# The second matrix product of a fused mLSTM cell and gated layer: seven half-width products in place of eight

## The chip, the cores and the metric

One core of a Trainium2 chip runs the whole program. The metric is device microseconds of one execution; the time of before is the median of three runs. Engines are named as in the profile: PE (matrix engine, with PEld for its weight loads), DVE (VectorE), ACT (ScalarE), POOL (GpSimd) and SP (the queue that issues most DMAs).

## The reference, cut to what matters

Two stages in float32. An mLSTM cell (4 batches, 8 heads, 768 steps, head size 40) gives `y`, which is laid out as `x` with 3072 rows and 320 columns. Then

```
h = x @ w_in          # (3072, 320) @ (320, 2048)
g = h * cos(h)
out = g @ w_out       # (3072, 2048) @ (2048, 320)
```

The cell is a recurrence over time; the kernel computes it in chunks of 128 steps, with a state carried from chunk to chunk. Only the last line, `g @ w_out`, is computed differently by the change. Both kernels compute it in float32.

## The kernel before

Time is cut into 6 chunks (c) of 128 steps, each for 4 batches (b). A chunk's layer has 16 blocks of 128 columns of `h` (NF = 16), two for each of 8 *slots* f2. Slot f2 = 2b + i of chunk c is one half of the body of `both_parts(c, b)`; the two slots of one b are called a pair here. In chunks 0 to 4 a pair also computes the cell of batch b for the next chunk (n = 4(c + 1) + b); chunk 5 has no cell left. In chunk 4 the cell no longer updates the state.

What PE runs in a pair, in the order in which the kernel writes it (all engines keep that order):

- first slot: `Up` (L605, L608: two tiles `pup` of 128x512 from `xT` and `w_in`), `scores` (ps, L462), `down` (po, L637), `values` (vt, L488 to L495);
- second slot: `Up`, `seam` (px, L563, which reads `yt`; and pu, L570), `down`.

`down(c, f2 - 1)` is the product with `w_out`: for two column blocks and four batches, 8 matmuls of 128x128 by 128x320, added up in four PSUM tiles `po` over the chunk. It runs one slot behind `Up`; the chunk's last one runs in the first slot of the next chunk, where ACT copies the four tiles out (L640) and SP stores them (L641).

What VectorE runs in a pair:

- first slot: L616 twice (after ACT's L613), `weigh` (L468 twice), `decay_exponents(n + 1)` (L387, followed on POOL by L388 and on ACT by the exponent L396), the gates L625 twice (they write `g` and set the `pup` tiles free), then `turn_gate` (oT, L440) and `normalize_turned` (L504 to L515), whose last instruction writes the third of `yt` that px reads;
- second slot: L616 twice, `state` (L588), the gates, then `turn_blocks` (L435 twice: `t`, which ps of the next pair reads).

POOL has besides L388: the multiplication into `xT` (L514), `fade` (L550), `weigh_k` (kw, L401) and `scale_q` (qG, L444, which values reads). ACT has L613, the sine L621, in the first pair of a chunk `sigmoid(c + 1)`, the exponents, and table loads between them.

In chunk 0 the kernel also brings in both weight matrices as 64-bit numbers and converts them to float32 on ACT, DVE and POOL (`to_float32`, L148 to L156).

```
        order = [(f, b) for f in (2 * f2, 2 * f2 + 1) for b in range(B)]
        for f, b in order:
            nc.tensor.matmul(po[c][b], gs[c, f][:, ts(b, C)], w_out_sb[:, f], start=(f == 0), stop=(f == NF - 1))
```

Of the kernel before, what the change touches and what calls it, by code (L numbers as in the profile page):

```python
# [29 lines left out]
def kernel(  # L30
# [23 lines left out]
    C = 128  # L54
# [16 lines left out]
    wp = ctx.enter_context(tc.tile_pool(name="wp", bufs=1))  # L71
    p2 = ctx.enter_context(tc.tile_pool(name="p2", bufs=2))
    p3 = ctx.enter_context(tc.tile_pool(name="p3", bufs=3))
    pe = ctx.enter_context(tc.tile_pool(name="pe", bufs=2))
    p1 = ctx.enter_context(tc.tile_pool(name="p1", bufs=1))
    pb = ctx.enter_context(tc.tile_pool(name="pb", bufs=4))
    pc = ctx.enter_context(tc.tile_pool(name="pc", bufs=3))
# [113 lines left out]
    M0 = gates.tile([BH, C], FP, name="M0")  # L191
    e0 = gates.tile([BH, C], FP, name="e0")
    nM = gates.tile([BH, 1], FP, name="nM")
    a1 = gp.tile([128, WQ], FP, name="a1", tag="g")[0:BH].rearrange("r (c s) -> r c s", c=R)
    F1 = gp.tile([128, WQ], FP, name="F1", tag="g")[0:BH].rearrange("r (c s) -> r c s", c=R)
    M1 = gp.tile([128, WQ], FP, name="M1", tag="g")[0:BH].rearrange("r (c s) -> r c s", c=R)

    keep = gp.tile([128, WQ], FP, name="keep", tag="g")[0:BH].rearrange("r (c s) -> r c s", c=R)
    shift = gp.tile([128, WQ], FP, name="shift", tag="g")[0:BH].rearrange("r (c s) -> r c s", c=R)
    m0 = gates.tile([BH, R], FP, name="m0")  # L200
    dd = gates.tile([BH, R - 1, BH], FP, name="dd")
    nc.gpsimd.memset(keep, 1.0)
# [140 lines left out]

    def load_E(n):
        c, b = divmod(n, B)
        E = pe.tile([128, 2, H, C], FP, name="E", tag="E") if n % 2 == 0 else E2[n // 2]
        if n % 2 == 0:
            E2[n // 2] = E
        if c > 0:
            src = M_d[1][b * H:(b + 2) * H, ts(c - 1, C)]  # L350
            nc.sync.dma_start(out=E.rearrange("q b h t -> q (b h) t"), in_=src.unsqueeze(0).to_broadcast([128, 2 * H, C]))
            Es[n + 1] = E[:, 1]
            G = p2.tile([128, 2 * HP, C], FP, name="G", tag="G")
            src = G_d.rearrange("(b p j) t -> j (b p) t", j=2, p=HP)
            for j in range(2):
                nc.sync.dma_start(out=G[64 * j:64 * j + 64], in_=src[j, 4 * b:4 * b + 8, ts(c - 1, C)].unsqueeze(0).to_broadcast([64, 2 * HP, C]))
            Gs[n], Gs[n + 1] = G[:, 0:HP], G[:, HP:2 * HP]
        elif n not in SPREAD:
            nc.sync.dma_start(out=E[:, n % 2], in_=M_d[0][ts(b, H)].unsqueeze(0).to_broadcast([128, H, C]))
        Es[n] = E[:, n % 2]  # L360

    E2 = {}
    pm = {}

    def wall_in(n, i, m):
# [227 lines left out]
    class Up:  # L593
# [27 lines left out]
            nc.scalar.activation(out=r, in_=r, func=AF.Sin, scale=TWO_PI_DOWN)  # L621

        def gate(self, e):
            g = gp.tile([128, WQ], FP, name="g", tag="g")[:, 0:B * C]
            nc.vector.scalar_tensor_tensor(out=g, in0=self.pu[e], scalar=TWO_PI, in1=self.n[e].bitcast(FP),  # L625
                                           op0=OP.mult, op1=OP.mult)
            gs[self.c, 2 * self.f2 + e] = g

    def down(c, f2):
        if f2 == 0:  # L630
            po[c] = [ps_o.tile([128, DM], FP, name="po", tag="o") for _ in range(B)]

        order = [(f, b) for f in (2 * f2, 2 * f2 + 1) for b in range(B)]
        if f2 == NF // 2 - 1:
            order.sort(key=lambda fb: fb[1])
        for f, b in order:
            nc.tensor.matmul(po[c][b], gs[c, f][:, ts(b, C)], w_out_sb[:, f], start=(f == 0), stop=(f == NF - 1))  # L637
            if f == NF - 1:
                o = p2.tile([128, DM], FP, name="o_sb", tag="o_sb")
                nc.scalar.copy(out=o, in_=po[c][b])  # L640
                nc.sync.dma_start(out=out[b * S + c * C:b * S + (c + 1) * C], in_=o)  # L641


    pw, pmu = (ps_u.tile([128, HP, C], FP, name=name, tag="up") for name in ("pw", "pmu"))

# [5 lines left out]
    def first_cells():  # L651
        nc.vector.memset(nil, 0.0)
        gates_in()
        nc.scalar.copy(out=ident_b, in_=ident)
        load(0, "qk")
        later_gates_in()
        load(0, "v")
        load(1, "qk")
        load_o(0, (0, 1))
        load(1, "v")  # L660
        load(2, "qk")
        last_rows(0)
        load_E(0)
        load_E(1)
        warm(12)
        wall_in(0, 0, pmu)
        wall_in(0, 1, psum_o())
        gates_first()
        gates_first_out()
        spread(0, 0)  # L670
        decay_exponents_half(0, 0)
        turn(0)
        turn_out(0, False)
        gates_sums()
        spread(0, 1)
        decay_exponents_half(0, 1)
        decay(0)
        weigh_k(0)
        load_E(2)
        load(2, "v")  # L680
        load_E(3)
        load_o(0, (2, 3))
        load(3)
        pieces.extend(weights_in(0))
        wall_in(1, 0, psum_o())
        wall_in(1, 1, psum_o())
        gates_less_sums()
        spread(1, 0)
        decay_exponents_half(1, 0)
        scores(0)  # L690
        gates_maxima()
        turn(1)
        weigh(0)
        sigmoid(0, slice(0, 2))
        turn_out(1, False)
        spread(1, 1)
        decay_exponents_half(1, 1)
        gates_exponents()
        decay(1)
        weigh_k(1)  # L700
        values(0)
        normalize(0)
        scores(1)
        gates_exp()
        turn(2)
        turn_out(2, False)
        warm(2)
        seam(0)
        weigh(1)
        seam_out(0)  # L710
        state(0)
        load_two(B, "qk")
        decay_exponents(2)
        gates_diagonal()
        decay(2)
        weigh_k(2)
        values(1)
        load_E(B)
        last_rows(1)
        load_o(1)  # L720
        outs.append((0, weights_out(0)))
        normalize(1)
        scores(2)
        turn(3)
        sigmoid(0, slice(2, 4))
        seam(1)
        load_two(B, "Kv")
        weigh(2)
        decay_exponents(3)
        turn_out(3)  # L730
        seam_out(1)
        values(2)
        decay(3)
        weigh_k(3)
        state(1)
        normalize(2)
        scores(3)
        pg = gates_turn()
        warm(1)
        seam(2)  # L740
        weigh(3)
        to_float32(*pieces.pop(0))
        pieces.extend(weights_in(1))
        outs.extend((p, weights_out(p)) for p in range(1, 3))
        seam_out(2)
        state(2)
        gates_keep(*pg)
        values(3)
        normalize(3)
        turn_blocks(B)  # L750
        to_float32(*pieces.pop(0))
        warm(3)
        seam(3)
        seam_out(3)
        to_float32(*pieces.pop(0))
        state(3)
        decay_exponents(B)
        load_two(B + 2)
        load_E(B + 2)
        decay(B)  # L760
        weigh_k(B)
        odd_values(B)
        scale_q(B)
        for f in range(2, NF // 4):
            last_rows(f)
# [14 lines left out]
    def both_parts(c, b):  # L780
# [3 lines left out]
        for i in range(2):  # L784
# [15 lines left out]
            if i == 0:  # L800
                if cell:
                    weigh(n)
                    if n + 1 < N:
                        decay_exponents(n + 1)
                for e in range(2):
                    up.sin(e)
                    up.gate(e)
                if b == 0 and c + 1 < NC:
                    sigmoid(c + 1)

                if c == 0 and b > 0 and pieces:
                    to_float32(*pieces.pop(0))
                if cell and n + 1 < N and (c > 0 or b > 0):
                    decay(n + 1)
            else:
                if cell:
                    seam_out(n)
                if pieces:
                    to_float32(*pieces.pop(0))
                if cell:  # L820
                    state(n)
                for e in range(2):
                    up.sin(e)
                    up.gate(e)
                while pieces:
                    to_float32(*pieces.pop(0))
                if cell and n + 1 < N:
                    weigh_k(n + 1)
                    odd_values(n + 1)
            if f2 > 0:  # L830
                down(c, f2 - 1)
            elif c > 0:
                down(c - 1, NF // 2 - 1)
            if cell and i == 0:
                turn_gate(n)
                values(n)
# [1 line left out]
                fade(n)  # L838
                if n % 2 == 1 and n + 3 < N:
                    load_two(n + 3, "qk")  # L840
                    load_E(n + 3)
                if b == B - 2 and c + 2 < NC:
                    load_o(c + 2)
# [6 lines left out]
            if i == 1:  # L850
                if c == 0 and b + 2 < B:
                    pieces.extend(weights_in(b + 2))
                for _ in range(min(2, len(outs))):
                    next_out()
                if cell and n + 1 < N:
                    turn_blocks(n + 1)
                    scale_q(n + 1)
# [2 lines left out]
    with tc.manual_schedule():  # L860
        first_cells()
        for c in range(NC):
            for b in range(B):
                both_parts(c, b)
        down(NC - 1, NF // 2 - 1)


# [28 lines left out]
```

## Time and profile before

| what | value |
|---|---|
| median of three runs | 583.64 us (581.65 to 583.67) |
| the profiled execution | 584.48 us |
| its span (first to last instruction) | 582.6 us |
| mean granted PE clock | 0.967 |
| PE, DVE, ACT, POOL busy | 553.2, 362.9, 257.1, 150.4 us |

The profile is of one execution. Its groups give the busy time and mean duration of instructions of one line; the chain of waits follows the work that ended last back to what released it; the timeline gives starts in microseconds from the first instruction. Durations of PE records overlap, so the cost of a matmul is the distance between starts. A float32 matmul appears as two records.

### The profile page before, as it was taken

The numbers are of one execution on the slowest core, as the hardware profiler recorded it, in microseconds if no ns is written. First come the engines' busy times: TensorE is split into PE (matmuls) and PEld (weight loads), VectorE is DVE, ScalarE is ACT, GpSimd is POOL, SyncE is SP. The second block draws the span as 40 slices with busy tenths as digits, with TensorE's granted clock in tenths as the row PEclk, the third lists the DMA queues.
The fourth block names the chain that finished last, engine by engine and source line by source line (L and its number), as shares of the span: only waits on it lengthen the run. The fifth ranks groups of instructions, "written<-read, shape, count | busy, mean of one in ns | idle before, by whom it ended". The sixth has DMA issues, their size and how long they took to land.

```text
span 582.6 us, 8973 instructions
## 1 busy us (share of the span) xinstructions
PE 553.2 (95%) x3404; PEld 325.7 (56%) x3404; DVE 362.9 (62%) x709; ACT 257.1 (44%) x419; POOL 150.4 (26%) x214
## 2 busy tenths in 40 slices
PE   8994959888999999999999999999999999999997
PEld 5862535444556556556556556566566565555454
DVE  5765798978676766766666667666566585423221
ACT  4856526373364344364343373353274251323222
POOL 7523454543231321321321321321211110000000
PEclk9868889997999999999999999999999999999999
DMA  9999999984805924914914914904810000010001
GB/s 149 221 220 216 229 246 228 198 191 90 153 26 112 161 41 91 154 44 93 160 41 90 154 46 92 182 18 90 154 47 2 0 1 1 0 45 1 0 1 45
DMA packets 125866, 58.76 MB, mean 101 GB/s; under 512 B 61648, under 2 KB 122144, under 8 KB 125824
## 3 DMA queue, kind: packets, MB, share of 16 engines
q1 hardware_dynamic: 125680, 58.00, 50.7%
q8 instruction: 27, 0.44, 0.3%
q0 software_dynamic: 96, 0.18, 0.1%
q14 instruction: 15, 0.12, 0.1%
q10 hardware_dynamic: 48, 0.02, 0.0%
HBM read 54.07 MB, written 5.16 MB: 102 GB/s over the span
## 4 chain that ended last, share of the span: by engine, by line
PE 85%; DVE 5%; DMA 5%; SPq 2%; POOL 2%; issue 1%; ACT 0%; POOLq 0%; DVEq 0%; ACTq 0%
PE po L637 35%; PE pup L605 27%; PE pup L608 8%; PE ps L462 4%; PE vt L495 2%; PE vt L488 2%; DMA E<-M_d 2%; DMA o<-in_o_gate_dram 1%; PE px L563 1%; PE pu L570 1%; DMA ks<-in_k_dram 1%; SPq L140 1%; PE ph L478 1%; PE pt L425 1%; DVE w_out_sb L153 1%
## 5 line engine op out<-in xcount | busy, mean ns | idle before, releaser
L637 PE MATMUL po<-w_out_sb,g 128*128 128x320 f32 x768 | 223.1, 445 | 1.0 <-POOL w_out_sb L156 1.0
L637 PEld LDWEIGHTS po<-w_out_sb,g 128*128 128x128 f32 x768 | 144.5, 193 | 65.8 <-issue 9.5
L605 PE MATMUL pup<-xT,w_in_sb 128*128 128x512 f32 x384 | 176.8, 602 | 1.0 <-POOL w_in_sb L156 0.7
L616 DVE SCALAR_TENSOR_TENSOR n<-pup,n 128x512 f32<-128x512 f32 x96 | 61.7, 685 | 157.6 <-ACT n L613 157.5
L613 ACT ACTIVATE n<-pup 128x512 int32<-128x512 f32 x96 | 51.9, 592 | 235.6 <-PE pup L608 235.6
L605 PEld LDWEIGHTS pup<-xT,w_in_sb 128*128 128x128 f32 x384 | 71.7, 192 | 80.3 <-issue 67.0
L621 ACT ACTIVATE n<-n 128x512 f32<-128x512 f32 x96 | 58.6, 630 | 17.4 <-DVE n L616 15.4
L625 DVE SCALAR_TENSOR_TENSOR g<-pup,n 128x512 f32<-128x512 f32 x96 | 61.6, 684 | 1.7
L388 POOL TENSOR_SCALAR_AFFINE_SELECT E<-E 128x1024 f32<-128x1024 f32 x22 | 24.0, 1092 | 129.2 <-DVE E L387 129.2
L608 PE MATMUL pup<-xT,w_in_l 64*128 64x512 f32 x192 | 54.2, 641 | 0.4 <-POOL w_in_l L156 0.4
L444 POOL TENSOR_TENSOR qG<-t,G 128x512 f32<-128x512 f32 x20 | 25.4, 1272 | 67.3 <-DVE t L435 61.7
L514 POOL TENSOR_TENSOR xT<-yt,db 128x256 f32<-128x256 f32 x20 | 14.5, 725 | 92.7 <-DVE db L511 92.7
L396 ACT ACTIVATE E<-E 128x1024 f32<-128x1024 f32 x24 | 25.4, 1060 | 29.3 <-POOL E L388 28.1
L462 PEld LDWEIGHTS ps<-t,t 40*128 40x128 f32 x384 | 26.5, 199 | 21.0 <-issue 17.8
L462 PE MATMUL ps<-t,t 40*128 40x128 f32 x384 | 28.1, 288 | 10.4 <-DVE t L435 10.4
L608 PEld LDWEIGHTS pup<-xT,w_in_l 64*128 64x128 f32 x192 | 14.4, 184 | 36.8 <-issue 34.9
L468 DVE TENSOR_TENSOR E<-ps,E 128x512 f32<-128x512 f32 x48 | 30.7, 680 | 2.4 <-PE ps L462 2.4
L396 ACT ACT_TABLE_LOAD x21 | 26.9, 1283 | 0.4
L387 DVE TENSOR_TENSOR E<-E,tab 128x1024 f32<-128x1024 f32 x22 | 26.7, 1214 | 0.0
L495 PE MATMUL vt<-qG,st 128*32 128x128 f32 x480 | 24.9, 280 | 0.8 <-POOL qG L444 0.8
L772 ACT ACT_TABLE_LOAD x19 | 24.4, 1283 | 0.2
L550 POOL TENSOR_TENSOR st<-st,tab 40x128 f32<-40x128 f32 x64 | 24.1, 395 | 1.2
(140 smaller groups left out, 510.7 us busy)
## 6 DMA issues: line engine op xcount, KB each, us to landing
E<-M_d SPq DMA_DIRECT2D x10, 1024.0 KB, 5.7
qr<-in_q_dram SPq DMA_DIRECT2D x40, 160.0 KB, 3.5
kr<-in_k_dram SPq DMA_DIRECT2D x40, 160.0 KB, 4.8
G<-G_d SPq DMA_DIRECT2D x20, 256.0 KB, 6.8
bits<-in_moe_w_out_dram SPq DMA_DIRECT2D x8, 640.0 KB, 6.6
bits<-in_moe_w_in_dram SPq DMA_DIRECT2D x32, 128.0 KB, 4.6
out_dram<-o_sb SPq DMA_DIRECT2D x24, 160.0 KB, 1.8
o<-in_o_gate_dram SPq DMA_DIRECT2D x40, 80.0 KB, 3.8
```

The costliest lines, as they stand in the source:

```text
L387: nc.vector.tensor_tensor(out=E, in0=E, in1=cols(n, 0, C), op=OP.subtract)
L396: nc.scalar.activation(out=Es[n], in_=Es[n], func=AF.Exp, scale=-1.0)
L462: nc.tensor.matmul(ps[j][:, p], kT[r, p], qT[r, p], start=True, stop=True)
L468: nc.vector.tensor_tensor(out=w, in0=pss[n][j], in1=w, op=OP.mult)
L495: nc.tensor.matmul(vt[32 * a:32 * a + 32, i], state[:, ts(HP * i + a, 32)], Gs[n][:, a], start=False, stop=True)
L605: nc.tensor.matmul(pu, w_in_sb[:, i, ts(2 * f2 + e, 128)], x(i), start=(i == 0), stop=False)
L608: nc.tensor.matmul(pu, w_in_l[r, f2], x(NK, r), start=False, stop=True)
L613: nc.scalar.activation(out=self.n[e], in_=self.pu[e], func=AF.Copy, bias=0.25)
L616: nc.vector.scalar_tensor_tensor(out=self.n[e].bitcast(FP), in0=self.pu[e], scalar=0.25, in1=self.n[e], op0=OP.add, op1=OP.subtract)
L621: nc.scalar.activation(out=r, in_=r, func=AF.Sin, scale=TWO_PI_DOWN)
L625: nc.vector.scalar_tensor_tensor(out=g, in0=self.pu[e], scalar=TWO_PI, in1=self.n[e].bitcast(FP), op0=OP.mult, op1=OP.mult)
L637: nc.tensor.matmul(po[c][b], gs[c, f][:, ts(b, C)], w_out_sb[:, f], start=(f == 0), stop=(f == NF - 1))
```

## The change

From chunk 1 on, the product with `w_out` is computed by blocks of two by two. For a pair of batches (p), the rows are the two batches, the inner blocks the two column blocks of a slot, and the columns of `w_out` the two halves of 160. Instead of eight products of such blocks, seven are made, of sums and differences of blocks:

- `weight_sums` (POOL) makes three sums of blocks of `w_out` (T2, T3, T4) and overwrites one block (T1): four subtractions of 128x640 at the end of chunk 0 and four in the first slot of chunk 1.
- `sums` (DVE) makes, in every slot from chunk 1 on, the sums of the blocks of `g`: seven instructions of 128x128 (one of them 128x2x128) after the two gates.
- `products` gives 14 matmuls of 128x128 by 128x160 for a slot's two column blocks (7 for each p). They are added up in 14 accumulators of 160 columns, three to a PSUM tile. For chunks 1 to 4 two of the 14 are put off: `late_products` makes them for all of the chunk at once, 16 matmuls, in the second slot of the next chunk. In chunk 5 they are made with the others.
- `down_slot` says how many products a slot runs: chunk 0 as before; in chunk 1 12 from the second slot on; in chunks 2 to 4 12 in the first slot (the last of the chunk before), 16 late ones in the second, 14 in each of the others; in chunk 5 16 or 17 in each of the others, and 14 at the very end.
- `combine` (one ACT copy and five or three DVE additions for each p) and `combine_late` (three additions) make the outputs from the accumulators. For the chunk before, `combine` stands on DVE in the chunk's first slot behind `sums` and ahead of `turn_gate`, `combine_late` in the second slot.
- Buffers: the exponents' tile E is loaded for one batch at a time (three buffers, the fourth of the start in another pool) and not for two; the output tiles have four buffers; the scratch of the gates' start lies in buffers that are idle then.

```diff
-    pe = ctx.enter_context(tc.tile_pool(name="pe", bufs=2))
+    pe = ctx.enter_context(tc.tile_pool(name="pe", bufs=3))
+    po_s = ctx.enter_context(tc.tile_pool(name="po_s", bufs=4))
...
-    a1 = gp.tile([128, WQ], FP, name="a1", tag="g")[0:BH].rearrange("r (c s) -> r c s", c=R)
...
+    spare = [raws[w][1][0:BH, x:x + WQ] for w in "qk" for x in (0, WQ)]
+    spare.append(pc.tile([128, 2 * WQ], FP, name="spare", tag="bits")[0:BH, 0:WQ])
+    a1, F1, M1, keep, shift = (t.rearrange("r (c s) -> r c s", c=R) for t in spare)
...
+            E = pe.tile([128, H, C], FP, name="E", tag="E")
...
-            nc.sync.dma_start(out=E.rearrange("q b h t -> q (b h) t"), in_=src.unsqueeze(0).to_broadcast([128, 2 * H, C]))
+            nc.sync.dma_start(out=E, in_=M_d[1][ts(b, H), ts(c - 1, C)].unsqueeze(0).to_broadcast([128, H, C]))
...
+    def weight_sums(part):
...
+        B11, B12, B21, B22 = (wv[:, r, e, h] for e in range(2) for h in range(2))
+        T2, T3, T4 = (t[:, r] for t in T)
+        nc.gpsimd.tensor_tensor(out=T3, in0=B22, in1=B12, op=OP.subtract)
+        nc.gpsimd.tensor_tensor(out=B12, in0=B12, in1=B11, op=OP.subtract)
+        nc.gpsimd.tensor_tensor(out=T2, in0=B22, in1=B12, op=OP.subtract)
+        nc.gpsimd.tensor_tensor(out=T4, in0=B21, in1=T2, op=OP.subtract)
+
+    def sums(c, k):
+        if k % 4 == 0:
+            Ds[c, k // 4] = pb.tile([128, 4, 2, C], FP, name="D", tag="bits")
+        D1, D4 = (Ds[c, k // 4][:, k % 4, i] for i in range(2))
+        S = Ss[c, k] = p2.tile([128, 4, C], FP, name="S", tag="S")
+        G0, G1 = (gs[c, 2 * k + e].rearrange("q (p e t) -> q p e t", p=2, e=2) for e in range(2))
+        tt = nc.vector.tensor_tensor
+        tt(out=S[:, 2], in0=G0[:, 0, 1], in1=G1[:, 0, 1], op=OP.add)
+        tt(out=D1, in0=G0[:, 1, 1], in1=G1[:, 1, 1], op=OP.add)
+        tt(out=G0[:, :, 1], in0=G0[:, :, 0], in1=G0[:, :, 1], op=OP.subtract)
+        tt(out=S[:, 0], in0=S[:, 2], in1=G0[:, 0, 0], op=OP.subtract)
+        tt(out=S[:, 1], in0=D1, in1=G0[:, 1, 0], op=OP.subtract)
+        tt(out=S[:, 3], in0=G1[:, 0, 0], in1=S[:, 0], op=OP.subtract)
+        tt(out=D4, in0=G1[:, 1, 0], in1=S[:, 1], op=OP.subtract)
+
+    def products(c, k):
...
+        made = [(X0, 0, G0[:, 0, 0], B11), (X0, 1, G1[:, 0, 0], B21), (X0, 2, S[:, 0], T2),
+                (Y0, 0, G0[:, 0, 1], T3), (Y0, 1, G1[:, 0, 1], T4), (Y0, 2, S[:, 2], T1),
+                (Y1, 2, S[:, 3], B22),
+                (X1, 0, G0[:, 1, 0], B11), (X1, 1, G1[:, 1, 0], B21), (X1, 2, S[:, 1], T2),
+                (Y1, 0, G0[:, 1, 1], T3), (Y1, 1, G1[:, 1, 1], T4)]
+        if c == NC - 1:
+            made += [(L, 0, D1, T1), (L, 1, D4, B22)]
...
+    def combine(c, p):
...
+        nc.scalar.copy(out=s[:, 0:HALF], in_=X[:, 0])
+        tt(out=o[0].rearrange("q (h n) -> q h n", h=2), in0=X[:, 1:3], in1=s[:, 0:HALF].unsqueeze(1).to_broadcast([128, 2, HALF]), op=OP.add)
+        if p == 0:
+            tt(out=s[:, HALF:DM], in0=Y[:, 0], in1=o[0][:, HALF:DM], op=OP.add)
...
+    def down_slot(c, f2):
...
+        if f2 == 0:
+            if c == 1:
+                down(0, LAST)
+            else:
+                run(made_of[c - 1], 12)
+                combine(c - 1, 0)
+                combine(c - 1, 1)
+            return
+        if f2 == 1 and c > 1:
+            run(late_products(c - 1), NF)
+            combine_late(c - 1)
+            return
...
@@ both_parts, in either slot
                 for e in range(2):
                     up.sin(e)
                     up.gate(e)
+                if c > 0:
+                    sums(c, f2)
...
-            if f2 > 0:
-                down(c, f2 - 1)
-            elif c > 0:
-                down(c - 1, NF // 2 - 1)
+            down_slot(c, f2)
+            if (c, f2) == (1, 0):
+                weight_sums(1)
...
+                if (c, f2) == (0, LAST):
+                    weight_sums(0)
...
@@ the end of the kernel
-        down(NC - 1, NF // 2 - 1)
+        run(made_of[NC - 1], 14)
+        for p in range(2):
+            combine(NC - 1, p)
+        combine_late(NC - 1)
```

## The prediction

> **What bounds the kernel now.** First the page: engine shares, granted clock, the chain's shares, the costliest groups.
>
> ```profile
> PE 553.2 (95%) x3404; PEld 325.7 (56%) x3404; DVE 362.9 (62%) x709; ACT 257.1 (44%) x419; POOL 150.4 (26%) x214
> ...
> PEclk9868889997999999999999999999999999999999
> ...
> PE 85%; DVE 5%; DMA 5%; SPq 2%; POOL 2%; issue 1%; ACT 0%; POOLq 0%; DVEq 0%; ACTq 0%
> ...
> L637 PE MATMUL po<-w_out_sb,g 128*128 128x320 f32 x768 | 223.1, 445 | 1.0 <-POOL w_out_sb L156 1.0
> ```
>
> From chunk 1 on TensorE is the chain, at full clock. An fp32 matmul is two records, so one w_out group of 8 matmuls is 16. What one costs is read from the chain of waits inside chunk 3:
>
> ```profile
> 272.50 4.50 PE po L637 x16
> ...
> 278.67 3.63 PE pup L605 x8
> ...
> 283.36 0.42 PE px L563 x2
> ...
> 288.75 1.29 PE pup L605 x3
> ```
>
> A pair of slots (one b) takes 21.64 us in chunks 1 to 3, 20.97 in chunk 4 and 2 x 9.0 in chunk 5. So removing PE work helps only as long as nothing PE waits for is late. The timeline of the same pair shows the tightest of these, the chain on VectorE that ends at yt (L515), which px (L563) reads:
>
> ```profile
> 272.26 1.29 DVE L616 SCALAR_TENSOR_TENSOR n<-pup,n 128x512 f32<-128x512 f32 x2 [4.02 <-ACT n L613]
> ...
> 275.80 1.28 DVE L625 SCALAR_TENSOR_TENSOR g<-pup,n 128x512 f32<-128x512 f32 x2
> ...
> 277.00 0.97 DVE L440 STREAM_TRANSPOSE oT<-og 128x384 f32<-128x384 f32 x1
> ...
> 278.73 0.29 DVE L504 TENSOR_SCALAR dt<-vt 128x128 f32<-128x128 f32 x1 [0.77 <-PE vt L495]
> 279.06 0.29 DVE L505 SCALAR_TENSOR_TENSOR dt<-vt,dt 128x128 f32<-128x128 f32 x1
> ...
> 281.45 0.71 DVE L515 TENSOR_TENSOR yt<-yt,db 128x128 f32<-128x128 f32 x1
> ...
> 283.29 0.49 PE L563 MATMUL px<-yt,pick 128*128 128x128 f32 x2
> ```
>
> Count from the pair's first L616 (272.26). yt is ready at 9.9 and PE gets to px at 11.02: slack 1.1. From px to the next pair's first L616 is 21.64 - 11.02 = 10.62, all PE and a fixed 0.6 of ACT.
>
> **PE's saving.** Of the 4.50, 16 x 0.269 = 4.31 is streaming; pup gives 3.43/8 = 0.429 at 512 columns. The line through both is 0.00083 us a column, so 160 columns take 0.136 us if the weight load stays hidden. The timeline of the startup bounds that, where only 41 columns move per load:
>
> ```profile
> 15.71 1.86 PEld L478 LDWEIGHTS ph<-vs,E 128*128 128x128 f32 x16
> ```
>
> 1.86/16 = 0.116 us per load, under 0.136, although one load lasts 193 ns in the groups: loads overlap. I take 0.136; the bounds are 0.136 and 0.193. A slot of 14 products costs 28 x 0.136 = 3.81 for 4.31, -0.50; of 12 (chunk 1, and each chunk's first slot) -1.04; the 16 put-off ones +0.04. In all 5 x (128 x 0.269 - 224 x 0.136) = -20 us.
>
> **The sums.** Seven additions per slot, on VectorE behind the two L625, ahead of oT. No group shows this operation alone; steps come from neighbours. After a 128-element operation an independent one starts 0.21 later (279.06 to 279.27), a dependent one 0.33 (278.73 to 279.06). With dependence at the first (0.11 beyond issue) and third (0.31), and 256 elements in the third (0.34): 0.11 + 0.21 + 0.31 + 0.34 + 4 x 0.21 = 1.81 us. Bounds 1.5 (none waits) and 2.3 (each waits); 1.81 since only these wait. In the second slot of a pair they hide: t is then made at 18.4 (11.2 for L616, 3.3 to the L625 end, 1.8, 2.0 for both transposes), some 2 us before ps needs it. In the first they push oT from 4.73 to 6.54; L504 no longer waits for vt but starts at 7.36, yt is ready 3.43 later at 10.8 and px starts at 10.85. PE, now early, gets there at 10.5 (chunks 2 to 4) or 10.0 (chunk 1), and waits. New pair: 10.85 + 10.62 - 0.50 = 20.97, -0.67 on 21.64 (chunk 4 likewise on its own 20.97); in chunk 1 10.85 + 10.62 - 1.04 = 20.43, -1.21. Free would be sums of up to 1.5 us. sums also waits until PE has read S of two slots before: that read is at most the tenth product of the slot, 3 us in, before the L625 end: nothing.
>
> **Combination.** In the first slot of chunks 2 to 4, eight additions stand between sums and oT. The first waits for a copy on ACT, queued there behind sigmoid's and the exponent's table loads; the exponent (L396) ends at 257.72, 7.09 after that pair's L616 (250.62), so it starts at 7.09 + 0.3 + 0.05 = 7.45. Their steps: PSUM 128x320 0.44 (L528), 160 columns 0.32 (between L504's 0.29 and L507's 0.55 at 384), five of the eight wait for the one before (0.03 each): 2.9 us. oT at 10.35, yt at 14.6, px at 14.65, and behind px stand pu, the put-off products and the next pup. PE is there at 10.0 and idles 4.7 us. Pair 14.65 + 10.62 + 0.05 = 25.3: +3.7, thrice. The four ACT copies of before, 4 x 0.43, were covered and bring nothing. The three late additions (0.75) fall in the second slot, hidden.
>
> An idle of 4.7 us has a second price. In the rows of the chain at 138 us PE had idled 2.62 us, and then ps took 2.08 for 0.89 and po 6.68 for 4.50; the stretch table agrees:
>
> ```profile
> 130.00:138.00 8.00, 5.44 (x15) 1.93 (x13) 7.83 (x12) 2.63 (x5) 4.49 (x5) 1.00 0.00 0
> 138.00:145.00 7.00, 6.59 (x25) 4.82 (x26) 5.80 (x9) 3.39 (x4) 2.35 (x3) 0.51 1.01 187
> ```
>
> Granted clock 0.51 for 7 us: 3.3 us lost. Idles of 2.1 and 2.2 us (at 123, 109) cost none; those of 5.5 and 6.8 did. So +3.3 per long idle, bounds 0 and 3.4. The Trainium skill (TensorE: Matmul & The Clock Gate, HAM oscillation) ties the drop to a window of idle over 3.4 us and books 1.67 us of half clock, 0.83 lost, for each; by it the sum below would be 10 us less, 596. The row at 138 speaks against both figures.
>
> **Weight sums.** Eight POOL subtractions of 128x640, twice four, in the last slot of chunk 0 and the first of chunk 1. What they do to VectorE, from the two timelines at 79 us:
>
> ```profile
> 79.04 1.68 POOL L156 TENSOR_TENSOR w_out_sb<-w_out_sb,bits 128x640 int32<-128x640 int32 x1 [0.81 <-DVE w_out_sb L155]
> ...
> 79.35 1.73 DVE L153 TENSOR_SCALAR w_out_sb<-w_out_sb 128x640 int32<-128x640 int32 x1
> ```
>
> That L153 alone takes 0.50 (104.65): it waited until POOL was done. The second four start when POOL's affine select ends, just as sums begins, with two SBUF inputs each. Around 97 to 100 us the engines alternate one for one, so three of sums' seven sit between POOL's four (1.5 us each; L253 with 640 elements took 1.26, L156 1.6). The first four hold L387 for 1.0 us, so all this starts at 5.8: 5.8 + 4 x 1.5 + 3 x 0.28 + 4 x 0.21 = 13.4 for the end of sums instead of 6.5, and px comes at 13.4 + 0.82 + 3.43 + 0.05 = 17.8 with rounding. Idle 6.8, then the clock: 17.8 + 10.62 - 1.04 + 3.3 - 21.64 = +9.0. If VectorE were never held: -0.2. fade and xT are queued behind on POOL; state then still follows L616: nothing. qG, behind the first four, has 8 us to spare.
>
> **Rest.** Chunk 5 has no px; its PE time is 140 x 2 x 0.136 for 144 x 0.269, -0.7, sums hidden (4.4 us of VectorE in 9). The end: before, the last store is issued 0.8 us after PE; now five additions (1.8 us) and two stores follow, +1.5. E comes in 20 loads of half the size, odd cells' later in SP's queue but still a pair ahead: 0, bounds -2.5 (512 KB at 200 GB/s, in the loaded chunk 0) and +2. Stores now wait on VectorE at SP; what is queued behind is loads for two pairs on: 0. The gates' scratch moves to other buffers long free: 0.
>
> **Sum.** 3 x -1.21 + 9 x -0.67 + 3 x (3.7 + 3.3) + 9.0 - 0.7 + 1.5 = +21.2. The profiled execution took 584.48 (span 582.6), 0.8 above the median of 583.64: 605.7 like for like, 605 as a median. With the bounds (no POOL turns, other sums) this case spans 596 to 611.
>
> **Rivals.** (1) PE's chain stays covered: VectorE idles 38% of the span, and if yt is on time everywhere the kernel takes 584.5 - 20 + 1.5 = 566. It decides below 1.5 us of insertion before oT; the combination alone is 2.9, so I give it 0.12. (2) The waits are there, but the clock holds and POOL gives way: -3.6 - 6.0 + 11.1 - 0.2 - 0.7 + 1.5 = +2.1, 587: 0.18; for it, idles of 2.1 us cost no clock. (3) Each sum waits for the one before, 2.3 us: 0.5 x 16 more, 613: 0.04. (4) Weight loads bind at 0.193: 28 x 0.193 = 5.4 for 4.31, 40 x 1.1 = +44, 628; L478's rows say no: 0.02. My forecast: 0.64.
>
> **How the numbers follow.** 605 is the forecast's; 584 to 613 leaves out (1), a little of (2), and (4). A measurement tells 0.5% (2.9 us) from no change: faster 0.13 (rival 1 and a rest), same 0.09 (half of rival 2), slower 0.78.
>
> **What would show it.** Spacing 0.136 in the products; px waiting for yt 0.3 us in common pairs, over 4 in the first pair of chunks 1 to 4, each with a clock near half after it. The forecast is wrong if px hardly waits, if the idle leaves the clock at 1.00, or if VectorE's sums in chunk 1's first slot are not stretched by POOL.

## The result, and the profile after

The changed kernel takes 598.17 us (median of 4 runs, 597.32 to 602.17); the kernel before took 583.65 us beside it. The ratio is 1.026, 95% interval [1.021, 1.032]: slower. The profiled execution took 597.53 us with a span of 595.8, against 584.48 and 582.6. That is 13.1 us where the prediction's sum had 21.2; the forecast was 605 us with a range of 584 to 613.

Line numbers from here on are those of the changed kernel, mostly one lower than before: Up is L604 and L607, the layer's first step on ACT L612 and on DVE L615, the gates L624, oT L439, yt L514, px L562; the sums are L673 to L679, the weight sums L660 to L663, the products L712, the combination's copy L728 and its first addition L729.

The page of the changed kernel, engine shares, granted clock and the chain that ended last:

```profile
PE 546.0 (92%) x3884; PEld 370.1 (62%) x3884; DVE 453.1 (76%) x1044; ACT 251.7 (42%) x409; POOL 163.8 (27%) x222
...
PEclk8578879998987999999999998999998999999999
...
PE 45%; DVE 33%; DMA 8%; ACT 5%; SPq 4%; issue 2%; POOL 1%; DVEq 0%; ACTq 0%; POOLq 0%
```

PE is busy for 7 us less in a longer span, and VectorE, 5% of the chain before, is now a third of it. The clock row has new 8s behind the startup. The chain inside a common pair of chunk 3 (start, duration, what) shows where VectorE entered:

```profile
316.25 3.43 PE pup L604 x8
...
325.08 1.21 DVE g L624 x2
...
326.39 0.29 DVE S L673
...
327.95 0.20 DVE D L679
328.15 0.78 DVE oT L439
...
331.48 0.73 DVE yt L514
...
332.34 0.46 PE px L562 x2
...
333.27 4.00 PE acc L712 x28
```

Before, px followed pup on PE; now it follows yt. The sums stand between the gates and oT, and the 28 product records, 0.136 us apart, take 4.00 (28 x 0.136 and 0.19 for the first) where 16 records of `down`, 0.269 apart, took 4.50 (16 x 0.269 and 0.19). PE's waits from chunk 1 on are nearly one line (total, times, longest):

```profile
PE px L562 <- DVE yt L514: 25.2, 15, 5.9
PE vt L494 <- POOL qG L443: 0.6, 1, 0.6
```

px is late in fifteen of the sixteen pairs. A table of pairs tells what that costs. It gives, in us from one first Up to the next, the first pair of a chunk and the mean of its other three, from the two traces; "end" is chunk 5 to the end of the span.

| | before: first, others | after: first, others | chunk's change |
|---|---|---|---|
| chunk 0 (from the start) | 158.76 | 155.50 | -3.3 |
| chunk 1 | 21.64, 21.64 | 30.51, 20.40 | +5.2 |
| chunk 2 | 21.64, 21.64 | 26.89, 21.00 | +3.3 |
| chunk 3 | 21.64, 21.64 | 28.01, 21.00 | +4.5 |
| chunk 4 | 20.97, 20.97 | 26.34, 20.21 | +3.1 |
| end | 80.32 | 80.68 | +0.4 |

Every common pair is shorter; four first pairs give back more than all of them. In the first pair of chunk 2 the table of stretches (length, then busy time of PE, PEld, DVE, ACT, POOL, then the clock) reads:

```profile
259.00:262.60 3.60, 3.58 (x10) 1.06 (x8) 2.63 (x8) 1.99 (x4) 0.00 (x0) 1.00 0.00 0
262.60:267.30 4.70, 0.00 (x0) 0.02 (x1) 4.55 (x15) 1.55 (x4) 1.00 (x2) 0.99 0.59 181
267.30:270.60 3.30, 3.29 (x25) 2.97 (x26) 2.61 (x8) 1.31 (x3) 2.07 (x5) 0.50 0.00 0
271.00:274.00 3.00, 3.00 (x25) 3.00 (x24) 1.91 (x8) 0.00 (x0) 0.00 (x0) 1.00 0.00 0
```

PE stands still for 4.7 us while VectorE is busy, and then works 3.3 us at half clock. In the first pair of chunk 1, the timelines of VectorE and GpSimd (start, duration):

```profile
167.50 1.60 POOL L660 TENSOR_TENSOR T<-w_out_sb 128x640 f32<-128x640 f32 x1
169.18 1.54 POOL L661 TENSOR_TENSOR w_out_sb<-w_out_sb 128x640 f32<-128x640 f32 x1
170.80 1.60 POOL L662 TENSOR_TENSOR T<-w_out_sb 128x640 f32<-128x640 f32 x1
172.49 1.67 POOL L663 TENSOR_TENSOR T<-w_out_sb,T 128x640 f32<-128x640 f32 x1
```

```profile
167.59 1.66 DVE L674 TENSOR_TENSOR D<-g 128x128 f32<-128x128 f32 x1
169.29 1.72 DVE L675 TENSOR_TENSOR g<-g 128x256 f32<-128x256 f32 x1
170.93 1.63 DVE L676 TENSOR_TENSOR S<-S,g 128x128 f32<-128x128 f32 x1
172.48 0.28 DVE L677 TENSOR_TENSOR S<-D,g 128x128 f32<-128x128 f32 x1
172.68 1.62 DVE L678 TENSOR_TENSOR S<-g,S 128x128 f32<-128x128 f32 x1
```

An addition of 0.28 us (0.42 for L675) takes 1.6 to 1.7 when a GpSimd instruction runs beside it: each of the four long ones here ends 0.14 to 0.29 us after that instruction ends, and L677 slips in between two.

### The profile page after: what moved, and what is told of

Read it like the earlier page. It is cut to its first block, busy times and chain, and to the rows that moved or that the text cites. A ratio compares the mean times of both kernels' runs of the same rounds, so it can differ in the third digit from the quotient of the medians.

```text
span 595.8 us, 10295 instructions
## 1 busy us (share of the span) xinstructions
PE 546.0 (92%) x3884; PEld 370.1 (62%) x3884; DVE 453.1 (76%) x1044; ACT 251.7 (42%) x409; POOL 163.8 (27%) x222
## 4 chain that ended last, share of the span: by engine, by line
PE 45%; DVE 33%; DMA 8%; ACT 5%; SPq 4%; issue 2%; POOL 1%; DVEq 0%; ACTq 0%; POOLq 0%
PE pup L604 15%; PE acc L712 15%; PE pup L607 5%; PE late L712 4%; DVE n L615 3%; DVE g L624 3%; DMA bits<-in_moe_w_in_dram 3%; DMA E<-M_d 3%; PE po L636 3%; DVE E L386 2%; DVE E L467 2%; DVE dt L507 2%; DVE oT L439 2%; DVE yt L514 2%; DVE db L510 2%
## 5 line engine op out<-in xcount | busy, mean ns | idle before, releaser
L604 PE MATMUL pup<-xT,w_in_sb 128*128 128x512 f32 x384 | 175.7, 600 | 0.9 <-DVE g L624 0.5
L612 ACT ACTIVATE n<-pup 128x512 int32<-128x512 f32 x96 | 52.0, 592 | 233.4 <-PE pup L607 233.4
L615 DVE SCALAR_TENSOR_TENSOR n<-pup,n 128x512 f32<-128x512 f32 x96 | 61.7, 684 | 85.5 <-ACT n L612 85.3
L604 PEld LDWEIGHTS pup<-xT,w_in_sb 128*128 128x128 f32 x384 | 70.1, 191 | 75.5 <-issue 65.0
L620 ACT ACTIVATE n<-n 128x512 f32<-128x512 f32 x96 | 58.3, 629 | 15.3 <-DVE n L615 14.1
L624 DVE SCALAR_TENSOR_TENSOR g<-pup,n 128x512 f32<-128x512 f32 x96 | 61.8, 686 | 2.2 <-ACT n L620 0.6
L712 PE MATMUL acc<-w_out_sb,g 128*128 128x160 f32 x320 | 60.2, 310 | 0.0
L712 PE MATMUL acc<-T,g 128*128 128x160 f32 x320 | 58.6, 303 | 0.0
L607 PE MATMUL pup<-xT,w_in_l 64*128 64x512 f32 x192 | 54.2, 641 | 0.4 <-POOL w_in_l L157 0.4
L712 PEld LDWEIGHTS acc<-w_out_sb,g 128*128 128x128 f32 x320 | 48.4, 193 | 4.0 <-issue 2.3
L712 PEld LDWEIGHTS acc<-T,g 128*128 128x128 f32 x320 | 48.4, 192 | 2.0 <-issue 1.5
L636 PE MATMUL po<-w_out_sb,g 128*128 128x320 f32 x128 | 41.4, 481 | 2.9 <-POOL w_out_sb L157 2.9
L461 PEld LDWEIGHTS ps<-t,t 40*128 40x128 f32 x384 | 27.4, 205 | 20.4 <-issue 20.2
L607 PEld LDWEIGHTS pup<-xT,w_in_l 64*128 64x128 f32 x192 | 14.4, 184 | 36.8 <-issue 34.9
L712 PE MATMUL acc<-T,S 128*128 128x160 f32 x160 | 35.6, 304 | 0.0
L636 PEld LDWEIGHTS po<-w_out_sb,g 128*128 128x128 f32 x128 | 26.4, 212 | 14.7 <-issue 3.8
L562 PE MATMUL px<-yt,pick 128*128 128x128 f32 x40 | 10.5, 349 | 25.7 <-DVE yt L514 25.6
```

Source lines behind the costliest of these rows:

```text
L461: nc.tensor.matmul(ps[j][:, p], kT[r, p], qT[r, p], start=True, stop=True)
L604: nc.tensor.matmul(pu, w_in_sb[:, i, ts(2 * f2 + e, 128)], x(i), start=(i == 0), stop=False)
L607: nc.tensor.matmul(pu, w_in_l[r, f2], x(NK, r), start=False, stop=True)
L612: nc.scalar.activation(out=self.n[e], in_=self.pu[e], func=AF.Copy, bias=0.25)
L615: nc.vector.scalar_tensor_tensor(out=self.n[e].bitcast(FP), in0=self.pu[e], scalar=0.25, in1=self.n[e], op0=OP.add, op1=OP.subtract)
L712: nc.tensor.matmul(a, lhs, rhs, start=start, stop=stop)
```

## The experiments

The theory: PE did save its 20 us, and more was lost again because yt comes late (behind the sums and, once a chunk, the combination; in chunk 1 behind sums that GpSimd stretches) and because the clock drops behind the longest of these waits. Since the length of chunk 0 differs from run to run, each result also gives "from chunk 1", the time from chunk 1's first Up to the end in the profiled run: 423.9 before, 440.3 after.

**1. The combination behind yt**

```diff
-                combine(c - 1, 0)
-                combine(c - 1, 1)
+                if c == NC - 1:
+                    combine(c - 1, 0)
+                    combine(c - 1, 1)
...
                 normalize_turned(n)
+                if f2 == 0 and c > 1:
+                    combine(c - 1, 0)
+                    combine(c - 1, 1)
```

> The same instructions as the changed kernel; in the first slot of chunks 2 to 4 the combination stands behind the chain to yt instead of ahead of it. Theory (the first pairs of chunks 2 to 4 are long, 26.9, 28.0 and 26.3 us, because yt stands behind the combination on VectorE): TensorE's idle before px falls from 4.7 to about 0.6 us, the granted clock no longer drops there, and some of the delay comes back at the next Up, whose accumulators VectorE now releases 1 to 2 us late; first pairs of about 22.3, so 14 us in all: about 584 us against 598. Rival (these pairs are long for a reason of their own, the accumulators' hand-over or the transfers at a chunk's start): px is as late as before, 595 to 598.

Measured: 587.0 us (ratio to before 1.006 [1.003, 1.009]), from chunk 1 429.0. First pairs of chunks 2 to 4: 23.2, 23.2, 22.5 for 26.9, 28.0, 26.3 (about 22.3 was expected), with no drop of the clock in them; the second pairs rose from 20.96 to 21.36 (chunk 4 from 20.30 to 20.69). PE's waits in chunk 2's first pair:

```profile
PE pup L604 <- DVE g L624: 1.5, 1, 1.5
PE px L562 <- DVE yt L514: 0.8, 1, 0.8
```

The wait of 4.7 at px is gone and 1.5 of it comes back at the next Up, as expected. The order of VectorE's work, not the amount, made these pairs long.

**2. The sums behind yt**

```diff
-                if c > 0:
+                if c > 0 and not cell:
                     sums(c, f2)
...
                 normalize_turned(n)
+                if c > 0:
+                    sums(c, f2)
```

> The same instructions as the changed kernel; in every first slot that has a cell, the seven sums stand behind the chain to yt instead of ahead of it. Theory: px no longer waits 0.82 us in chunk 1's common pairs and 0.3 in those of chunks 2 to 4, but the sums then stand ahead of the next rest and gate: 20.4 becomes 19.7 and 20.97 about 20.8. In chunk 1's first pair the sums are what GpSimd's weight sums stretch; the chain to yt has one operation with two operands from SBUF, so px comes some 5 us earlier and the clock drop behind it shrinks: 30.5 becomes about 23. The first pairs of chunks 2 to 4 do not gain, because the combination there starts with ScalarE's copy at 7.0, and lose 0.5 each. Together about 588 us. Rival (every VectorE operation is held while GpSimd runs, whichever it is): chunk 1's first pair stays above 29 and the time at 594 or more.

Measured: 590.0 us (1.010 [1.006, 1.013]), from chunk 1 430.2. Chunk 1's first pair is 23.67, and its common ones 20.2 to 20.4, where 19.7 was expected: px waits no more there, but the next L615 and gates are later and the pair keeps its length. Chunks 2 to 4: 20.65 to 20.78 (chunk 4 19.97), first pairs 27.5, 27.0, 26.3: px still waits 4.7 us in them. VectorE in chunk 1's first pair, while GpSimd runs the four weight sums from 172.0 to 178.6:

```profile
173.17 0.55 DVE L506 TENSOR_TENSOR yt<-vt,oT 128x384 f32<-128x384 f32 x1
173.63 0.94 DVE L507 RECIPROCAL dt<-dt 128x128 f32<-128x128 f32 x1
...
175.36 1.61 DVE L514 TENSOR_TENSOR yt<-yt,db 128x128 f32<-128x128 f32 x1
176.89 0.28 DVE L673 TENSOR_TENSOR S<-g 128x128 f32<-128x128 f32 x1
177.09 1.64 DVE L674 TENSOR_TENSOR D<-g 128x128 f32<-128x128 f32 x1
```

L506, which reads one operand from PSUM, and the one-operand L507 run at their usual 0.55 and 0.94 beside GpSimd; L514 (0.7 elsewhere) and L674, with two operands from SBUF, take 1.6. That refutes the rival that every VectorE instruction is held. The Trainium skill (SBUF — State Buffer, "SBUF: two separate sides") names an exclusive lock, held for the whole instruction, between GpSimd and a VectorE instruction that has two inputs in SBUF or runs in a two-port mode. The two rows of 1.6 us agree with its first case. Two inputs in SBUF are not the only case: L153 of the kernel before, with one tensor as input, took 1.73 us for 0.50 beside a GpSimd instruction (the rows at 79 us in the prediction).

**3. Half of the weight sums on VectorE**

```diff
-            if (c, f2) == (1, 0):
-                weight_sums(1)
...
                     scale_q(n + 1)
+                if (c, f2) == (1, 1):
+                    weight_sums(1, nc.vector)
```

> The second part of the weight sums (four instructions) runs on VectorE at the end of chunk 1's second slot, behind the next cell's transposes, instead of on GpSimd at the end of the first slot. Theory (GpSimd's weight sums hold VectorE's sums, which makes yt and px late, and the idle before px drops the clock): the seven sums of chunk 1's first slot take 1.8 us again instead of 8.4, the idle before px falls from 5.9 to 1 or 2 us, the 10 us at half clock go, and the pair takes about 21.5 instead of 30.5; the four instructions on VectorE, some 3 us, lie mostly in its idle time while TensorE makes the next Up, at a cost of 0 to 1.5. Together about 589 us. Rival (the pair is long because the first part of the weight sums makes qG late, or because of the change of product at that place): 596 to 598.

Measured: 596.1 us (1.020 [1.015, 1.025]), from chunk 1 436.4. Chunk 1's first pair is 22.22, where about 21.5 was expected and the changed kernel had 30.51, so GpSimd's sums made it long. The total alone would not have told: it lies in the rival's range, because two losses took back half of these 8.3 us. First, the second pair is 23.15 instead of 20.4, a loss of 2.75 where 0 to 1.5 was expected. The last of the four instructions on VectorE, and what waits behind it:

```profile
186.40 0.82 DVE L662 TENSOR_TENSOR T<-w_out_sb 128x640 f32<-128x640 f32 x1
187.26 0.82 DVE L663 TENSOR_TENSOR T<-w_out_sb,T 128x640 f32<-128x640 f32 x1
188.00 1.28 DVE L615 SCALAR_TENSOR_TENSOR n<-pup,n 128x512 f32<-128x512 f32 x2
```

L615 starts late, px then waits 1.76 us instead of 0.82, and a drop of the clock follows this short idle:

```profile
197.00:198.80 1.80, 0.04 (x3) 0.04 (x1) 1.72 (x9) 1.09 (x2) 1.03 (x2) 1.00 1.40 162
198.80:200.20 1.40, 1.40 (x22) 1.22 (x23) 1.40 (x4) 0.91 (x3) 1.25 (x5) 1.00 1.36 120
200.20:203.60 3.40, 3.40 (x15) 3.40 (x15) 3.27 (x12) 0.40 (x1) 1.05 (x2) 0.50 0.60 101
```

0.94 more of wait and 1.7 of clock are all but 0.1 of the 2.75. Second, the drops in chunks 2, 3 and 4 lasted 6.83, 3.41 and 6.83 us in this run, where the changed kernel had 3.41, 6.83 and 3.41 behind the same waits of 4.73 us; nothing was changed there, and these chunks took 1.7 us more.

**4. The idle time filled, the wait left**

```diff
-            px = pool.tile([128, C], FP, name="px", tag=tag)
+            if n % B == 0 and n > 2 * B:
+                px = pool.tile([128, HP, C], FP, name="px", tag=tag)
+                warm(18, px)
+                px = px[:, 0]
+            else:
+                px = pool.tile([128, C], FP, name="px", tag=tag)
```

> In the first pairs of chunks 2 to 4, 18 idle bf16 matmuls of 128x512 (about 0.213 us each at full clock, 3.8 us) stand before px in px's own bank, inside the 4.7 us in which TensorE waits for yt; nothing else is changed and px waits as long as before. Theory (the idle itself costs 4.7 a pair, and the clock that drops behind it another 1.6 to 3): the granted clock stays at 1.00 behind these three pairs and they take 25.3, 25.3 and 24.9 instead of 26.9, 28.0 and 26.3: 592 us. Rival (the clock drops there for another cause, or the longer pairs are waits that the records do not show): same lengths, 598 us.

Measured: 594.2 us (1.017 [1.013, 1.021]), from chunk 1 432.7. First pairs 25.36, 25.36 and 24.68; expected were 25.3, 25.3 and 24.9. PE's timeline (px is L567 in this kernel) and the stretch behind it:

```profile
261.93 4.06 PE L788 MATMUL px<-nil 128*128 128x512 bf16 x18
266.66 0.49 PE L567 MATMUL px<-yt,pick 128*128 128x128 f32 x2 [0.67 <-DVE yt L514]
```

```profile
266.70:270.50 3.80, 3.80 (x39) 3.62 (x40) 3.67 (x11) 1.31 (x3) 2.12 (x5) 1.00 0.00 0
```

px still waits for yt, and the clock stays at 1.00. So the wait costs 4.4 us a pair more than a common pair's, and the clock 1.5, 2.7 and 1.7 on top, 5.8 us in all: two prices, each measured alone. From chunk 1 on this run is 7.5 us shorter than the changed kernel's; the other 1.6 are chunk 1's first pair, 28.91 for 30.51, where nothing was changed and half clock lasted 6.83 us for 10.24 behind the same wait.

**5. The products alone**

```diff
-        T2, T3, T4 = (t[:, k] for t in T)
+        T2, T3, T4 = B21, B22, B21
+        S = [G0[:, 0, 0], G0[:, 1, 0], G1[:, 0, 0], G1[:, 1, 0]]
+        S = {i: t for i, t in enumerate(S)}
...
-                    sums(c, f2)
+                    pass
```

> Left out: the sums, the weight sums and the combination; the same products read quarters of g and of w_out as they stand, and four ScalarE copies take each chunk's accumulators out, as the kernel before did. Theory (TensorE's work alone falls by the 20 us of the sum; all else is what VectorE and GpSimd put in its way): pairs of 19.6 in chunk 1, about 20.6 in chunks 2 and 3 and 20.0 in chunk 4, first pairs within 1 us of these, no clock drop behind chunk 0: about 566 us. Rival (the products cost more than 0.136 us a record in the long run, by their weight loads or by banks that are handed over late): pairs stay at 21 and more and the time at 575 or above.

Measured: 561.9 us (0.961 [0.958, 0.964]), from chunk 1 404.7. Pairs of 19.55, 20.63 and 19.97, first pairs the same except chunk 1's 20.59, whose first slot still runs the old product; no wait of PE from chunk 1 on. The page's first line:

```profile
PE 537.7 (96%) x3884; PEld 362.3 (65%) x3884; DVE 362.0 (65%) x709; ACT 259.1 (46%) x424; POOL 150.6 (27%) x214
```

404.7 against 423.9 is -19.2, for -20 in the sum and some 1 us given back at the end. PE's saving is real to the microsecond, and neither weight loads nor banks take from it. The median lies 4 us below the 566 expected; the profiled run's chunk 0 was 155.1 us long, for 158.8 before. In the changed kernel 440.3 - 404.7 = 35.6 us are lost to the rest: 20.0 in the first pairs of chunks 2 to 4, 9.9 in chunk 1's, 5.5 in the common pairs, 0.2 at the end.

**6. Buffers and loads**

```diff
-            down_slot(c, f2)
+            if f2 > 0:
+                down(c, f2 - 1)
+            elif c > 0:
+                down(c - 1, LAST)
```

> The changed kernel's buffers and its E loads, one cell each, with the w_out product of the kernel before; no sums, weight sums or combination. Theory (chunk 0's -3.3 us in the changed kernel's profile was one startup among others: five runs of the same startup reached chunk 1 at 155.5, 156.5, 157.8, 159.3 and 160.0 us): pairs of 21.64 and 20.97 as before, and 583.5 us within 2. Rival (the smaller E loads end the startup sooner and are a real part of the result): 580.4 us.

Measured: 581.9 us (0.996 [0.992, 0.999]), within the theory's 2 us but towards the rival, with the pairs of before. Two more runs were to settle it. The kernel before with its E loads split:

```diff
-            src = M_d[1][b * H:(b + 2) * H, ts(c - 1, C)]
-            nc.sync.dma_start(out=E.rearrange("q b h t -> q (b h) t"), in_=src.unsqueeze(0).to_broadcast([128, 2 * H, C]))
+            for i in range(2):
+                src = M_d[1][ts(b + i, H), ts(c - 1, C)]
+                nc.sync.dma_start(out=E[:, i], in_=src.unsqueeze(0).to_broadcast([128, H, C]))
```

> The kernel before with one edit: each E load of two cells is issued as two loads of one cell at the same place (the second one's issue comes 8 cells' rows later in SP's queue, no tile or wait is changed). Theory (the 1.9 us that buffers_alone gained are the startup's loads: with half of the size, cell 4's E is there sooner): about 582 us, pairs of 21.64 as before. Rival (E loads do nothing; buffers_alone's gain is the gates' scratch in other buffers, or chance): 583.8 us.

Measured: 584.9 us (1.002 [0.999, 1.004]): the size of the loads alone gains nothing. And the kernel with the changed buffers again:

> buffers_alone once more, to narrow its interval. Theory (its gain of 1.9 us is real): 581 to 583, the interval below 1. Rival (chance among startups of 155 to 161 us): 583 to 585, the interval around 1.

Measured: 582.9 us (0.998 [0.996, 1.001]). The buffers are worth between nothing and some 2 us; more is not settled. 0.6 us can be read: the end took 79.73 us in both traces, for 80.32 before. What is shown is the scatter: over eleven profiled runs with the changed buffers, chunk 1's first Up came at 155.1 to 160.9, mean 157.8; the two with the old ones had 158.8 and 160.1. The changed kernel's 155.5 lies at the low end.

**7. A version that is faster**

First, experiments 1 and 2 together:

> The combination and the sums both stand behind the chain to yt (the sums first, then the combination). Theory (the chain to yt, not VectorE's total, made px late): in the first pairs of chunks 2 to 4 yt is 1.8 us earlier than with the combination alone moved, px waits no more, the next rest comes about 1.4 earlier, and the pairs take 21.6 to 22 instead of 23.2, the common ones 20.65 to 20.9; chunk 1 as with the sums moved (23.7, then 20.3). With 157.8 for chunk 0 (the mean of five runs of one startup) and 80.65 for the end: 84.6 + 2 x 84.3 + 82.0 + 238.5 + 1.8 = 575 us. Rival (VectorE's work in these pairs, some 22 us of it, is the bound by now, so that what is moved only waits elsewhere): first pairs stay at 23.2, 580 or more.

Measured: 581.3 us (0.996 [0.993, 0.999]), from chunk 1 421.6. First pairs 24.1, 24.1 and 21.9, not 21.6 to 22; the time is the rival's (580 or more). PE's waits in chunk 2 give a reason other than VectorE's total:

```profile
PE pup L604 <- DVE g L624: 2.1, 2, 1.6
PE late L712 <- DVE o_sb L729: 1.6, 1, 1.6
```

The put-off products (`late`) wait for the combination's first addition, which frees their bank and now stands behind the sums: px no longer waits, `late` does. The last version below tells the two reasons apart.

Second, the weight sums in four parts, put behind GpSimd's affine select:

```diff
-        r = ts(part, NF // 4)
+        r = ts(part, NF // 8)
...
                         decay_exponents(n + 1)
+                if c == 1:
+                    weight_sums(b)
```

> As both_later, and the weight sums run on GpSimd in four parts of two blocks instead of two of four, each behind the affine_select of a first slot of chunk 1, where VectorE's next operations read PSUM or one operand. Theory (GpSimd's weight sums cost nothing where VectorE does not run operations with both operands in SBUF and where qG is not queued behind them): in chunk 1's first pair qG starts with the transposes' end, no VectorE operation between the gates and yt takes over 1.3 us, and the pair takes about 20.5 instead of 23.7 (changed kernel: 30.5); the rest as both_later. About 572 us, so 2% faster than the kernel before. Rival (spread out, they hold VectorE four times): chunk 1's pairs of 21.5 or more each, 577 or more.

Measured: 578.6 us (0.991 [0.988, 0.995]), from chunk 1 419.5; the first pairs of chunks 2 to 4 as in the run above, which is the miss. Chunk 1's first pair is 21.12, where about 20.5 was expected and the run above had 23.68; its others are 20.43 to 20.57. GpSimd and VectorE there:

```profile
165.24 0.89 POOL L660 TENSOR_TENSOR T<-w_out_sb 128x320 f32<-128x320 f32 x1
...
168.10 0.87 POOL L663 TENSOR_TENSOR T<-w_out_sb,T 128x320 f32<-128x320 f32 x1
```

```profile
165.24 0.93 DVE L439 STREAM_TRANSPOSE oT<-og 128x384 f32<-128x384 f32 x1
...
169.68 0.77 DVE L514 TENSOR_TENSOR yt<-yt,db 128x128 f32<-128x128 f32 x1
```

The four fit between the gates and L514, where VectorE reads PSUM or one operand, and no instruction there is stretched. The sums behind L514 still meet GpSimd's other work: L678 takes 1.13 us beside kw (L400). Last, the combination in two halves:

```diff
-        s = p1.tile([128, 3 * C], FP, name="m", tag="db")
+        s = p1.tile([128, HALF], FP, name="m", tag="m")
...
                 normalize_turned(n)
+                if f2 == 0 and c > 1:
+                    combine(c - 1, 0)
+                if c > 0:
+                    sums(c, f2)
...
                     scale_q(n + 1)
+                if cell and f2 == 1 and c > 1:
+                    combine(c - 1, 1)
+                    combine_late(c - 1)
```

> As all_spread, with three moves for the chunk's first pair: ScalarE's copy of an accumulator goes to a tile of its own (before, the buffer of db), the first half of the combination stands behind yt and ahead of the sums, and its second half and the three additions of the put-off products stand behind the next cell's transposes in the second slot, where VectorE has some 2.5 us to spare. Theory (in all_spread the first pairs of chunks 2 and 3 take 24.07 us because the put-off products wait 1.6 for the bank that the first combination frees and the next Up 1.6 for gates that stand behind the whole of it): both waits go, first pairs of 20.7 to 21.3, second ones of 20.8 to 21.2, chunk 4 about 80.4 us instead of 82.5: 570 us. Rival (VectorE's total of some 22 us binds these pairs): first and second pairs keep their sum of 45.4 in chunks 2 and 3, 577 us or more.

Measured: 567.9 us (0.976 [0.971, 0.980]), from chunk 1 409.7. First pairs 21.1, 21.1 and 19.97, second ones 20.77, 20.78 and 19.98. This is faster than both kernels: it keeps 14.1 of the 19.2 us of PE's saving. Its page and all of PE's waits from chunk 1 on:

```profile
PE 541.6 (96%) x3884; PEld 363.8 (64%) x3884; DVE 459.5 (81%) x1044; ACT 252.1 (45%) x409; POOL 168.1 (30%) x230
```

```profile
PE pup L604 <- DVE g L624: 2.8, 6, 0.8
```

VectorE is busier than in the changed kernel (81% for 76%) and the kernel 30 us shorter. Its work did not bind; its order, and GpSimd's, did. First and second pairs of chunk 2 take 41.9 us together, not the 45.4 of the rival. What the copy's own tile adds was not tested apart.

## Why the prediction was right, and what it mis-sized

**PE's saving**, -20: right. Product records lie 0.136 us apart, and the products alone give -19.2 with the end included.

**The sums**, 1.81 us and 0.3 (chunk 1: 0.87) of wait at px: right. The timeline of VectorE shows the pair's first L615 and oT:

```profile
321.47 1.29 DVE L615 SCALAR_TENSOR_TENSOR n<-pup,n 128x512 f32<-128x512 f32 x2 [2.57 <-ACT n L612]
...
328.06 0.86 DVE L439 STREAM_TRANSPOSE oT<-og 128x384 f32<-128x384 f32 x1
```

oT starts 6.59 us after that L615, where 6.54 was worked out, and the chain has 1.76 from the first sum (326.39) to oT (328.15). px waits 0.3 and 0.82 and the pairs are 21.00 and 20.40, for 20.97 and 20.43. Chunk 4's others gained 0.76 instead of 0.67; its last pair waits less.

**The combination**, +3.7 of wait in three first pairs: right. In chunk 2's, px starts 14.77 us after the first L615 (14.65 was worked out) with 4.73 idle for 4.7:

```profile
252.54 1.29 DVE L615 SCALAR_TENSOR_TENSOR n<-pup,n 128x512 f32<-128x512 f32 x2 [2.50 <-ACT n L612]
...
267.31 0.76 PE L562 MATMUL px<-yt,pick 128*128 128x128 f32 x2 [4.73 <-DVE yt L514]
```

With the clock held (experiment 4) the pair takes 25.36, for 25.3. The combination's start behind ScalarE's exponent came at 7.30, for 7.45. The three late additions in the second slot hid, as costed.

**Weight sums on GpSimd**, +9.0: right, by its own steps. px starts 17.85 us after the first L615 (17.8), the pair is 30.51 for 21.64, +8.9. The sums end at 13.6, for 13.4. That it fits to 0.1 is partly luck: in experiment 4's run the same wait at px cost half as much clock and the pair took 28.91. One particular was wrong at no cost here: qG was said to have 8 us to spare, but the first four weight sums push it from about 158 to 164, and PE waits 0.6 us for it and then 5.9 at px, where the prediction had 6.8 at px alone.

**The clock behind the idles** is the step that failed in size. It was put at 3.3 us each, from one row at 138 us. In chunk 1 it was 3.3: half clock lasted 10.24 us, of which 6.6 remained after the idle. In chunks 2 to 4 it was 1.6, 2.8 and 1.6, 6.0 instead of 9.9. The stretches behind the idles of chunk 1 and chunk 3:

```profile
178.70:185.20 6.50, 6.50 (x37) 6.17 (x38) 5.74 (x16) 1.31 (x3) 2.03 (x5) 0.50 0.00 1
...
356.00:363.00 7.00, 5.80 (x35) 5.50 (x36) 6.08 (x18) 1.31 (x3) 3.08 (x6) 0.52 0.03 8
```

In chunk 3 px starts at 357.2, so of the 6.83 us at half clock 5.6 cost anything. Half clock lasts whole units of 3.41 us, and part of it can pass while PE is still waiting; a row that shows the drop gives its price only there. Experiment 4 puts the sum at 5.8. "Idles of 2.1 and 2.2 us cost none" is true of the trace it was read from, not in general: over all traces twelve idles of 2.1 to 2.3 us in chunk 0 began at full clock, and six of them ended in two units of half clock.

**Chunk 0**, 0 with bounds -2.5 and +2: measured -3.3, outside the bounds but inside the scatter of the eleven startups, so chance can give it; how much the buffers add is not settled. With the clock's -3.9 these are 7.2 of the 8 us by which the profiled sum was too long; the rest is chunk 4's pairs and 0.4 at the end (+0.4 for +0.8).

**The rivals.** "All covered", 566: PE's work alone is what experiment 5 shows (561.9). In the changed kernel yt is not on time, and this rival fails on the 2.9 us of the combination, as its point of decision said. "Clock holds and GpSimd gives way", 587, fails on both rows: the clock's 0.50 and the sums' 1.6 us. Sums of 2.3 us and bound weight loads are refuted by 1.76 us and by 0.136.

The Trainium skill's rule that was weighed (TensorE: Matmul & The Clock Gate, HAM oscillation), 0.83 us for an idle of over 3.4, would by the prediction's estimate have made 596, nearer to the result in total. That is luck: its parts do not hold here, since the three equal idles cost 1.6 to 2.8 each, the longer one 3.3, and one of 1.76 us cost 1.7.

## What to carry to other kernels

Work taken off the bounding engine is worth what that engine's latest input allows: list for each stage the slack of what it waits for, and put additions behind the instruction that releases the bounding engine, not ahead of it. A bulky step (here the combination) can be split, with the half that frees a bank early and the other in a gap. Keep GpSimd's instructions on SBUF out of the stretches in which VectorE runs instructions with two operands in SBUF (or ones like L153) that something waits for. And where a total agrees with a rival, look at the lengths of the stages before believing it: experiment 3's total did, and its pairs did not.

## What the runs showed of the hardware

- Half clock comes in units of 3.41 us (3.41, 6.83 or 10.24 behind the idles of this list). Nine idles of PE of 4.7 us before px (chunks 2 to 4 of the changed kernel and of experiments 2 and 3) were each followed by one or two units, beginning 2.2 to 5.0 us after the idle began; three of 5.9 us by two or three. Filled with matmuls, three such waits of 4.7 us brought none. Of ten idles of 1.53 to 1.76 us from chunk 1 on, two were followed by a unit, one of them at a price of 1.7 us. The same kernel's same wait can cost 1.6 or 2.8 us. The Trainium skill (TensorE: Matmul & The Clock Gate, "What's actually happening") has a free-running window of 3413 ns, which fits the units; an idle of a whole window, which it names as the condition, was not needed here.
- Where VectorE reads two operands from SBUF, GpSimd and VectorE trade turns one instruction at a time: seven additions of 1.8 us together took 7.8 beside a GpSimd affine select of 1.1 and four GpSimd subtractions of 1.6. A reciprocal, a shuffle, a transpose and an addition with one operand in PSUM kept their times (0.94, 0.30, 0.96 and 0.55 us). At 128x640 a subtraction takes 1.6 us on GpSimd and 0.82 on VectorE.
